# Weight conversion with low parts written in place, two mantissa tiles, a high-part tile of its own and one store for each part

## The chip, the cores and the metric

The kernel runs on one core of one Trainium2 chip. The metric is the device time of one execution in microseconds (us). The kernel before takes 964.32 us, the median of three runs (963.54 to 965.41).

## What is computed

Bucketed attention (queries and keys meet only where six sign bits agree) feeds a gated block. Cut to what matters:

```python
mask = q_bucket[:, :, :, None] == k_bucket[:, :, None, :]
scores = np.where(mask, scale * np.matmul(q, k.transpose(0, 1, 3, 2)), -1000000000.0)
attn = np.exp(scores - np.max(scores, axis=-1, keepdims=True))
attn = attn / (np.sum(attn, axis=-1, keepdims=True) + 1e-09)
x = np.matmul(attn, v)          # 4 batches, 8 heads, 768 positions, 64 wide; joined to 3072 x 512
gate = 1.0 / (1.0 + np.exp(-(x @ w_gate)))   # weights 512 x 1536, float64
out = (gate * (x @ w_val)) @ w_out           # 1536 x 512, float64
```

The three weight matrices arrive as float64, which no engine here computes with: the kernel reads them as pairs of 32-bit integers and makes float32 numbers of them, each of which it splits into a high part (rounded to the matmul format) and a low part (the rest).

## The kernel before

There are two phases. In **phase 1** (to about 405 us) a pair of heads at a time goes through attention: scores on TensorE (L1551, L1557), their maximum on VectorE (L1569, 192 times), the exponential on ScalarE (L1578), transposes on TensorE (L1614) whose results ScalarE or VectorE copies back (L1620), and the product with v (L1630). For each next pair, q and k are loaded, turned on TensorE (L1358), copied out (L1372 to L1378, on ScalarE or VectorE) and split into high and low parts (L1385 to L1389, on ScalarE, GpSimd or VectorE). In **phase 2** (from about 429 us) the gate and value products run in a seven-product scheme on blocks of weights (L1178) and the output products follow (L932). Between the two stands a short piece with ordinary products (L896, L932 with `zg`, `zv`, `zo`).

Beside attention the weights are converted, 34 items in phase 1 and six more early in phase 2. An item is a 128x512 block (for gate and value also three sums and one difference of its quarters, which make it 128x896). Its steps: a load of 512 KB into `raw` (L745, L748, L813); on VectorE `exponent` (L689) and `mantissa` (L697), on ScalarE `shifted` (L692), on VectorE `whole` (L702) and `signed` (L707); on GpSimd `scaled` (L712), `sums` (L821 to L824), `high` (L766 or L830) and `low` (L769 or L833); then a store to DRAM (L772 or L836), from where phase 2 fetches the weights (L1728, L777). The exponents lie in tile `wex`, the mantissas, later the finished float32 numbers, in tile `wmf`; high and low part go to one tile `wk` with two halves.

The order of the work is set by a planner (`Plan`, L380): each step is a task with a key; TensorE follows a list of task numbers (`ORDER`) and the other engines take the ready task with the smallest key (keys are moved by the table `SHIFT`). A task takes and gives counted resources (`stock`): `raw1` one load buffer, `mid1` one pair of `wex` and `wmf`, taken by `exponent` and given back by `low`; `wk` one tile, taken by `high` and given back when the store has landed. Some steps have two possible engines, and the planner takes the one that is free. Each engine then executes its own instructions strictly in the order that came out, and SyncE issues nearly all DMAs in the same way.

Of the kernel before, what the change touches and what calls it, by code (L numbers as in the profile page):

```python
# [19 lines left out]
P = 128  # L20
# [21 lines left out]
SLOTS = ("two", "one", "e", "st", "su", "sv", "rb", "xs", "vr", "h", "raw2")  # L42
# [465 lines left out]
def lsh_attention_glu_kernel(ctx, tc, q, k, v, proj, w_gate, w_val, w_out, out):  # L508
# [165 lines left out]
    def floats(key, load, after, last, name):  # L674
# [12 lines left out]
        def exponent():  # L687
            z["ex"] = stage().tile([P, N_EL], I32, name=f"ex{name}", tag="wex", bufs=stock["mid" + own])
            nc.vector.tensor_scalar(z["ex"], z["high"], 0x7FF00000, None, op0=ALU.bitwise_and)  # L689
# [45 lines left out]
    def load_w(key, n, j, early, last=None):  # L735
# [32 lines left out]
        def low(eng):  # L768
            eng.tensor_sub(z["w"][:, 1], f(z["mf"]), f(z["w"][:, 0]))  # L769
# [1007 lines left out]
```

## Time and profile before

| | |
|---|---|
| median of three runs | 964.32 us (963.54 to 965.41) |
| the profiled execution: its own time, its span | 965.6 us, 963.8 us |
| TensorE busy | 952.0 us, 99% of the span |
| VectorE, ScalarE, GpSimd busy | 608.2, 548.2, 274.3 us |
| granted TensorE clock, mean | 0.999 |

The page gives busy times of each engine and the chain of work that ended last; the same view can be asked of a stretch. A row of a group of instructions has its line in the code, engine, operation, output and inputs, shapes, count, then the busy time in us, the mean of one in ns, and the idle time of the engine just before them with what ended it. In a timeline a row has its start and duration in us; in brackets stands the idle time before it and its releaser. DVE is VectorE, ACT ScalarE, POOL GpSimd, PE TensorE, PEld its weight loads, SPq SyncE's queue.

### The profile page before, as it was taken

How to read it: one execution, taken by the hardware profiler on the slowest of the kernel's cores; microseconds unless marked ns; L12 is line 12 of the kernel's file. 1: busy time of each engine (PE TensorE's matmuls, PEld its weight loads, DVE VectorE, ACT ScalarE, POOL GpSimd, SP SyncE). 2: the span in 40 equal slices, each digit the busy share in tenths (PEclk: the TensorE clock that was granted, in tenths of full speed). 3: DMA queues.
4: the chain of work that ended last, by engine and by line, in shares of the span. 5: the costliest groups of instructions: out<-in, count | busy, mean ns of one | idle time of the engine just before them, and what ended most of it. 6: DMA issues, size and time to landing. Idle time of an engine off the chain costs nothing.

```text
span 963.8 us, 20105 instructions
## 1 busy us (share of the span) xinstructions
PE 952.0 (99%) x8067; PEld 774.8 (80%) x8070; DVE 608.2 (63%) x1173; ACT 548.2 (57%) x993; POOL 274.3 (28%) x325
## 2 busy tenths in 40 slices
PE   9999999999999999999999999999999999999998
PEld 5666665666666567689999999999999999999997
DVE  7999898999899898676656743334633336333332
ACT  5988898898888889554334433324433235333322
POOL 4444655666765665630000000000000000000000
PEclk9999999999999999999999999999999999999999
DMA  7666888888897877489966774444744444644421
GB/s 186 175 194 189 224 252 241 244 249 238 263 268 213 233 228 228 171 315 411 370 237 230 280 262 175 153 153 154 271 170 158 170 177 173 222 154 153 154 78 66
DMA packets 116606, 204.37 MB, mean 212 GB/s; under 512 B 63456, under 2 KB 87968, under 8 KB 110624
## 3 DMA queue, kind: packets, MB, share of 16 engines
q1 hardware_dynamic: 107456, 118.08, 39.9%
q0 software_dynamic: 6688, 84.42, 23.7%
q8 instruction: 63, 1.03, 0.4%
q10 hardware_dynamic: 2368, 0.59, 0.3%
q14 instruction: 31, 0.25, 0.1%
HBM read 147.84 MB, written 43.42 MB: 198 GB/s over the span
## 4 chain that ended last, share of the span: by engine, by line
PE 92%; DVE 4%; DMA 2%; ACT 1%; issue 1%; SPq 0%; ACTq 0%; DVEq 0%
PE y L932 20%; PE pv L1630 12%; PE zBg L1178 10%; PE zBv L1178 10%; PE sc L1557 9%; PE tp L1614 7%; PE zDv L1178 5%; PE zDg L1178 5%; PE sc L1551 4%; PE zAg L1178 2%; PE zAv L1178 2%; PE h L1452 1%; DVE e L1569 1%; PE zg L896 1%; PE zv L896 1%; PE idle L642 1%
## 5 line engine op out<-in xcount | busy, mean ns | idle before, releaser
L1569 DVE TENSOR_SCALAR_CACHE_REDUCE e<-sc 128x768 f32<-128x768 f32 x192 | 177.1, 952 | 20.3 <-PE sc L1557 18.5
L1578 ACT ACTIVATE e<-e,st 128x768 f32<-128x768 f32 x192 | 178.9, 933 | 15.1 <-DVE e L1569 13.2
L932 PE MATMUL y<-wo,gh 128*128 128x512 f32 x480 | 151.0, 396 | 0.0
L1630 PE MATMUL pv<-e,vr 128*64 128x384 f32 x768 | 140.7, 496 | 0.0
L1620 ACT COPY e<-tp 128x768 f32<-128x768 f32 x144 | 112.2, 795 | 27.9 <-PE tp L1614 27.1
L1614 PEld LDWEIGHTS tp<-ident,e 64*128 64x128 f32 x2304 | 87.0, 138 | 45.7 <-issue 13.7
L1178 PE MATMUL zBg<-x,wsg 128*128 128x384 f32 x552 | 111.0, 335 | 0.0
L1178 PE MATMUL zBv<-x,wsv 128*128 128x384 f32 x552 | 110.7, 335 | 0.0
L1178 PEld LDWEIGHTS zBg<-x,wsg 128*128 128x128 f32 x552 | 98.2, 188 | 6.6 <-ACT t1g L1186 0.4
L1178 PEld LDWEIGHTS zBv<-x,wsv 128*128 128x128 f32 x552 | 98.3, 188 | 6.0
L932 PEld LDWEIGHTS y<-wo,gh 128*128 128x128 f32 x480 | 89.9, 187 | 15.2
L1614 PE MATMUL tp<-ident,e 64*128 64x64 f32 x2304 | 99.6, 226 | 1.8 <-DVE e L1569 0.9
L1271 ACT CAST gh<-zt 128x384 fp32r<-128x384 f32 x92 | 47.1, 514 | 95.1 <-DVE zt L1266 75.5
L932 PE MATMUL y<-wo,gl 128*128 128x512 f32 x240 | 93.2, 388 | 0.0
L1557 PE MATMUL sc<-kh,ql 64*128 64x384 f32 x192 | 89.8, 468 | 0.0
L1557 PE MATMUL sc<-kh,qsl 64*128 64x384 f32 x192 | 89.8, 468 | 0.0
L1630 PEld LDWEIGHTS pv<-e,vr 128*64 128x64 f32 x768 | 48.2, 136 | 51.3 <-issue 43.0
L1728 POOL DMA_DIRECT2D wsv<-kzv x23 | 12.2, 532 | 236.9 <-PE zDg L1178 224.6
L1728 POOL DMA_DIRECT2D wsg<-kzg x23 | 12.3, 536 | 227.4 <-PE zDv L1178 206.9
L1250 ACT ACTIVATE sig<-sig 128x384 f32<-128x384 f32 x69 | 36.2, 525 | 61.7 <-DVE sig L1193 61.6
L1274 DVE TENSOR_TENSOR gl<-zt,gh 128x384 fp32r<-128x384 f32 x92 | 51.0, 554 | 29.2 <-ACT gh L1271 29.2
L1551 PE MATMUL sc<-kq 64*128 64x384 bf16 x384 | 64.8, 328 | 2.3 <-ACT e L1620 1.1
(214 smaller groups left out, 1964.4 us busy)
## 6 DMA issues: line engine op xcount, KB each, us to landing
wsg<-kzg POOLq DMA_DIRECT2D x23, 1792.0 KB, 8.1
wsv<-kzv POOLq DMA_DIRECT2D x23, 1792.0 KB, 7.6
kzg<-wkg SPq DMA_DIRECT2D x12, 896.0 KB
kzv<-wkv SPq DMA_DIRECT2D x12, 896.0 KB
rawg<-in_moe_w_gate_dram SPq DMA_DIRECT2D x14, 512.0 KB
rawv<-in_moe_w_val_dram SPq DMA_DIRECT2D x14, 512.0 KB
vr<-in_v_dram SPq DMA_DIRECT2D x16, 384.0 KB
rb<-rd SPq DMA_DIRECT2D x64, 96.0 KB
```

The costliest lines, as they stand in the source:

```text
L932: nc.tensor.matmul(acc, a[:, slot, ts_], w, start=(first and i == 0), stop=(last and i == 2), skip_group_check=cols != slice(None),)
L1178: nc.tensor.matmul(acc, streams[n, jp][:, c, wa, a_], X[x_][:, xa, c], start=first and c == 0 and i == 0, stop=c == 1 and i == 2, skip_gro ...
L1250: lambda blk=blk: nc.scalar.activation(sig[:, blk], w["B"][:, :GN] if blk == 2 else sig[:, blk], AF.Sigmoid),
L1271: nc.scalar.copy(side["h"][:, blk], w["z", blk])
L1274: eng.tensor_sub(side["l"][:, blk], w["z", blk], f(side["h"][:, blk]))
L1551: nc.tensor.matmul(sc[:, j, :GN], kq[z["h"]][rows, 2 + 2 * g + h, t * P : (t + 1) * P], kq[z["h"]][rows, h], start=True, stop=False, tile_ ...
L1557: nc.tensor.matmul(sc[:, j, :GN], q_[rows, c], z["k" + x][rows, h * GN : (h + 1) * GN], start=False, stop=(m == 2), tile_position=(j * D, 0),)
L1569: nc.vector.tensor_scalar(sp(e), gz["sc", t, h][:, :, :GN], -MASKED * SCALE, None, op0=ALU.min, op1=ALU.min, accum_out=gz["st", t][:, h : ...
L1578: nc.scalar.activation(e, e, AF.Exp, bias=st[:, h : h + 1], scale=-1.0, accum_out=gz["su"][:, h * GT + t : h * GT + t + 1],)
L1614: nc.tensor.transpose(tp[:, r, at_ : at_ + D], gz["e", t, h][rows, c * P : (c + 1) * P], ident[rows, rows], tile_position=(r * D, 0),)
L1620: copy(gz["e"][:, :, c * P : (c + 1) * P].rearrange("p n (r d) -> p r n d", r=2), gz["tp", c][:, :, :GN].rearrange("p r (n d) -> p r n d", ...
L1630: nc.tensor.matmul(gz["pv"][rows, :GN], z["v"][:, h, c], gz["e"][:, h * GT : (h + 1) * GT, c * P : (c + 1) * P], start=(c == 0), stop=(c = ...
```

## The change

Storage: `low` no longer writes the second half of `wk` but the tile that holds the mantissas, in place. `wk` keeps only the high part, half the size, and the space goes into a second `wmf` tile, so that the total is the same. The resource `mid1` now stands for the mantissa tiles alone and counts two; `exponent` takes a new resource `ex1` (one `wex` tile), given back by `scaled`; `mantissa` takes `mid1`, given back when the store of the low part has landed. `wk` is given back when the high part's store has landed and `low` has run. Each part has its own store of half the bytes: the high part can be stored while `low` still runs. The same for the six items of phase 2 (`mid2`, `ex2`, `wk2`). Blocks that stay on the chip (the first two of each matrix) keep their old places. The tables `ORDER` and `SHIFT` are new throughout (only their size is told here).

```diff
-SLOTS = ("two", "one", "e", "st", "su", "sv", "rb", "xs", "vr", "h", "raw2")
+SLOTS = ("two", "one", "e", "st", "su", "sv", "rb", "xs", "vr", "h", "raw2", "mid1", "mid2")
...
-        raw1=1, mid1=1, raw2=2, mid2=1, wk=1, xr=1, x2=1, x3=1, ob=3,
+        raw1=1, mid1=2, ex1=1, raw2=2, mid2=2, ex2=1, wk=1, xr=1, x2=1, x3=1, ob=3,
...
-            z["all"] = stage().tile([P, SL * P], I32, name=f"mf{name}", tag="wmf", bufs=stock["mid" + own])
+            z["all"] = stage().tile([P, SL * P], I32, name=f"mf{name}", tag=f"wmf{slot['mid' + own]}", bufs=1)
...
-        b1 = add(key, "dve", 336, exponent, after=[a], take=["mid" + own], port=0.92)
+        b1 = add(key, "dve", 336, exponent, after=[a], take=["ex" + own], port=0.92)
...
-        c1 = add(key, "dve", 400, mantissa, after=[b1], port=0.92)
+        c1 = add(key, "dve", 400, mantissa, after=[b1], take=["mid" + own], port=0.92)
...
-            eng.tensor_sub(z["w"][:, 1], f(z["mf"]), f(z["w"][:, 0]))
+            eng.tensor_sub(z["l"], f(z["mf"]), f(z["h"]))
...
-            y["w"] = stage().tile([P, 2, SL * P], F32R, name=f"wk{n}{jp}{c}", tag="wk", bufs=stock["wk"]).rearrange(
+            y["h"] = stage().tile([P, SL * P], F32R, name=f"wk{n}{jp}{c}", tag="wk", bufs=1).rearrange(
...
-            eng.tensor_sub(y["w"][:, 1], y["f"], f(y["w"])[:, 0])
+            y["l"] = y["f"].bitcast(F32R)
+            eng.tensor_sub(y["l"], y["f"], f(y["h"]))
...
-            nc.sync.dma_start(kept_z[n, jp][:, c], f(y["w"]))
+            nc.sync.dma_start(kept_z[n, jp][:, c, m], f(y["hl"[m]]))
...
-        keeps.setdefault((n, jp), []).append(dma(key, 917504, keep, after=[m], give=["wk2" if last else "wk"]))
+        s_ = [dma(key, 458752, lambda: keep(0), after=[h]), dma(key, 458752, lambda: keep(1), after=[m], give=["mid" + own])]
+        add(FIRST, "sp", 0, lambda: None, after=[s_[0], m], give=["wk2" if last else "wk"])
+        keeps.setdefault((n, jp), []).extend(s_)
```

Over the whole program TensorE has the same instructions in another order. The other engines differ in 32 more stores on SyncE, and in where the planner put the steps with two engines: VectorE has 5 copies of turned q fewer (`rawq`, ScalarE has 5 more), 1 copy of transposes fewer (`e<-tp`, ScalarE 1 more), 2 low parts of x fewer (`xl`, GpSimd 2 more), 1 low part of k more (`kl`, GpSimd 1 fewer), 1 low part of weights more (GpSimd 1 fewer), and 1 copy of a result in phase 2 fewer; 5 high parts of q and k moved from ScalarE to GpSimd.

VectorE at the border of the first and second batch, the place at which TensorE idles longest in phase 1; `e,st<-sc` are the maxima, `exg`, `mfg` the conversion, `e<-tp` a copy of transposes, `xs` the divided result, `kq` the bits. Before:

```order
L1569 TENSOR_SCALAR e_0_0_1996,st_0_0_0_1995<-sc_0_0_0_1_2036 128x768
L1569 TENSOR_SCALAR e_0_0_1996,st_0_0_1_2078<-sc_0_0_1_0_2052 128x768
L689 TENSOR_SCALAR exg_0_2097<-rawg_0_1933 128x512
L1620 COPY e_3_0_1570<-tp_3_0_5_2065 128x2x6x64
L697 TENSOR_SCALAR mfg_0_2131<-rawg_0_1933 128x512
L1569 TENSOR_SCALAR e_0_0_1996,st_0_0_2_2147<-sc_0_0_2_0_2121 128x768
L1569 TENSOR_SCALAR e_0_0_1996,st_0_0_1_2078<-sc_0_0_1_1_2108 128x768
L702 SCALAR_TENSOR_TENSOR mfg_0_2131<-rawg_0_1933,mfg_0_2131 128x512
L1637 TENSOR_TENSOR xs_3_0_2166<-pv_3_0_1922,rb_3_0_1915 128x384
L707 SCALAR_TENSOR_TENSOR exg_0_2097<-rawg_0_1933,exg_0_2097 128x512
L1458 TENSOR_SCALAR kq_209<-h_1_2159,thr,mul 128x384
```

And in the changed kernel, at the same maxima:

```order
L1611 TENSOR_SCALAR e_0_0_2070,st_0_0_0_2069<-sc_0_0_0_1_2039 128x768
L1420 TENSOR_SCALAR rawq_1_2120<-tq_1_2097 128x2x6x64
L1611 TENSOR_SCALAR e_0_0_2070,st_0_0_1_2140<-sc_0_0_1_0_2111 128x768
L860 TENSOR_TENSOR mfg_0_2036<-mfg_0_2036 128x128
L861 TENSOR_TENSOR mfg_0_2036<-mfg_0_2036 128x128
L862 TENSOR_TENSOR mfg_0_2036<-mfg_0_2036 128x128
L863 TENSOR_TENSOR mfg_0_2036<-mfg_0_2036 128x128
L1679 TENSOR_TENSOR xs_3_0_2170<-pv_3_0_1999,rb_3_0_1883 128x384
L1611 TENSOR_SCALAR e_0_0_2070,st_0_0_1_2140<-sc_0_0_1_1_2161 128x768
L1611 TENSOR_SCALAR e_0_0_2070,st_0_0_2_2202<-sc_0_0_2_0_2186 128x768
L717 TENSOR_SCALAR exg_1_2223<-rawg_1_2095 128x512
L1500 TENSOR_SCALAR kq_209<-h_1_2197,thr,mul 128x384
```

The exponent, the copy and the mantissa that stood in one piece between two maxima are gone from here; a copy of q and four short sums stand there instead, and the next item's exponent follows two maxima later.

GpSimd at the end of phase 1, the last items converted there; `gl` is the first step of the piece between the phases. Before:

```order
L712 TENSOR_TENSOR mfg_0_7506<-mfg_0_7506,exg_0_7500 128x512
L821 TENSOR_TENSOR mfg_0_7506<-mfg_0_7506 128x128
L822 TENSOR_TENSOR mfg_0_7506<-mfg_0_7506 128x128
L823 TENSOR_TENSOR mfg_0_7506<-mfg_0_7506 128x128
L824 TENSOR_TENSOR mfg_0_7506<-mfg_0_7506 128x128
L830 CAST wkg_7574<-mfg_0_7506 128x896
L833 TENSOR_TENSOR wkg_7574<-mfg_0_7506,wkg_7574 128x896
L920 TENSOR_TENSOR gl<-gf_0_0_7643,gh 128x384
```

And in the changed kernel:

```order
L869 CAST wkv_7513<-mfv_0_7397 128x896
L873 TENSOR_TENSOR mfv_0_7397<-mfv_0_7397,wkv_7513 128x896
L740 TENSOR_TENSOR mfo_7574<-mfo_7574,exo_7568 128x512
L798 CAST wo_7604<-mfo_7574 128x512
L801 TENSOR_TENSOR mfo_7574<-mfo_7574,wo_7604 128x512
L962 TENSOR_TENSOR gl<-gf_0_0_7674,gh 128x384
```

The last item is now a block of the output weights, which has no sums, and its low part overwrites `mfo`.

## Rows read from the trace of the kernel before

**Rows 1.** The page: busy time by engine, and the chain that ended last.

```profile
PE 952.0 (99%) x8067; PEld 774.8 (80%) x8070; DVE 608.2 (63%) x1173; ACT 548.2 (57%) x993; POOL 274.3 (28%) x325
PE 92%; DVE 4%; DMA 2%; ACT 1%; issue 1%; SPq 0%; ACTq 0%; DVEq 0%
```

**Rows 2.** Busy time by stage: stretch, length, engines (instructions), clock, DMA share, GB/s.

```profile
20.00:400.00 380.00, 374.74 (x4952) 246.46 (x4952) 343.53 (x691) 331.69 (x587) 225.52 (x242) 1.00 0.78 228
400.00:430.00 30.00, 28.75 (x187) 24.45 (x184) 17.79 (x22) 12.08 (x20) 14.49 (x19) 1.00 0.67 253
430.00:964.00 534.00, 529.97 (x2775) 492.56 (x2773) 232.20 (x420) 194.83 (x374) 23.85 (x44) 1.00 0.54 200
```

**Rows 3.** Waits of TensorE to 420 us: us in total, times, longest.

```profile
PE sc L1551 <- ACT e L1620: 1.1, 2, 0.9
PE h L1452 <- DVE xs L1637: 1.1, 1, 1.1
PE zo L932 <- DVE gl L920: 1.0, 1, 1.0
PE tp L1614 <- DVE e L1569: 0.9, 1, 0.9
```

**Rows 4.** Timeline, 103 to 114 us, four rows of four engines.

```profile
107.29 1.83 POOL L1389 TENSOR_TENSOR ql<-rawq,qh 128x768 fp32r<-128x768 f32 x1
...
107.31 2.09 DVE L697 TENSOR_SCALAR mfg<-rawg 128x512 int32<-128x512 int32 x1
...
110.31 0.94 ACT L1578 ACTIVATE e<-e,st 128x768 f32<-128x768 f32 x1 [1.19 <-DVE e L1569]
...
112.99 0.34 PE L1551 MATMUL sc<-kq 64*128 64x384 bf16 x2 [0.91 <-ACT e L1620]
```

**Rows 5.** Groups of instructions by shape to 425 us: steps that change engine.

```profile
L1378 DVE TENSOR_SCALAR rawq<-tq 128x768 f32<-128x768 f32 x8 | 7.6, 956 | 2.4 <-PE tq L1358 2.3
...
L1620 DVE COPY e<-tp 128x768 f32<-128x768 f32 x48 | 45.3, 951 | 5.2 <-PE tp L1614 5.1
...
L870 DVE TENSOR_TENSOR xl<-xr,xh 128x384 fp32r<-128x384 f32 x5 | 4.8, 979 | 0.4 <-POOL xh L867 0.4
...
L1389 DVE TENSOR_TENSOR kl<-rawk,kh 128x768 fp32r<-128x768 f32 x3 | 3.5, 1172 | 0.6 <-ACT kh L1385 0.6
```

**Rows 6.** The same view: the two conversion steps on VectorE with one input.

```profile
L697 DVE TENSOR_SCALAR mfv<-rawv 128x512 int32<-128x512 int32 x12 | 8.3, 688 | 0.0
...
L689 DVE TENSOR_SCALAR exg<-rawg 128x512 int32<-128x512 int32 x12 | 6.9, 575 | 0.0
...
L697 DVE TENSOR_SCALAR mfg<-rawg 128x512 int32<-128x512 int32 x12 | 6.7, 556 | 0.0
...
L689 DVE TENSOR_SCALAR exv<-rawv 128x512 int32<-128x512 int32 x12 | 6.4, 533 | 0.0
...
L689 DVE TENSOR_SCALAR exo<-rawo 128x512 int32<-128x512 int32 x10 | 6.2, 620 | 0.0
...
L697 DVE TENSOR_SCALAR mfo<-rawo 128x512 int32<-128x512 int32 x10 | 4.2, 420 | 0.0
```

**Rows 7.** Groups by shape: a low part on VectorE (430 to 964 us) and on GpSimd.

```profile
L833 DVE TENSOR_TENSOR wkv<-mfv,wkv 128x896 fp32r<-128x896 f32 x2 | 2.2, 1089 | 1.4 <-ACT wkv L830 1.4
...
L833 POOL TENSOR_TENSOR wkv<-mfv,wkv 128x896 fp32r<-128x896 f32 x10 | 22.3, 2227 | 0.8
```

**Rows 8.** Timeline, 204 to 220 us: load, end of one item, start of the next.

```profile
207.20 0.37 SPq L813 DMA_DIRECT2D rawv<-in_moe_w_val_dram  x1
...
213.28 2.11 POOL L833 TENSOR_TENSOR wkv<-mfv,wkv 128x896 fp32r<-128x896 f32 x1
...
215.95 0.42 DVE L689 TENSOR_SCALAR exv<-rawv 128x512 int32<-128x512 int32 x1
```

**Rows 9.** Stores of the gate weights on SyncE: ns min/median/max; and a wait there.

```profile
L836 SPq DMA_DIRECT2D kzg<-wkg x12: 320/346/1213, 105.8 to 496.1; - x12
...
SPq L1025 <- DMA kzg<-wkg: 3.5, 1, 3.5
```

More of the change, by code (lines that the diff above doesn't have):

```diff
@@ L687, in exponent @@
         def exponent():
-            z["ex"] = stage().tile([P, N_EL], I32, name=f"ex{name}", tag="wex", bufs=stock["mid" + own])
+            z["ex"] = stage().tile([P, N_EL], I32, name=f"ex{name}", tag="wex", bufs=1)
             nc.vector.tensor_scalar(z["ex"], z["high"], 0x7FF00000, None, op0=ALU.bitwise_and)
@@ L720, in floats @@
         return z, add(
-            key, "dve" if last else "pool", 680 if last else 1240, lambda: scaled(nc.vector if last else nc.gpsimd), after=[d], port=0.92
+            key, "dve" if last else "pool", 680 if last else 1240, lambda: scaled(nc.vector if last else nc.gpsimd), after=[d], give=["ex" + own], port=0.92
         ), own
@@ L764, in high, with keep, keep_both @@
             else:
-                z["w"] = stage1.tile([P, 2, SL * P], F32R, name=f"w{n}{j}", tag="wk", bufs=stock["wk"])[:, :, :N_EL]
-            (nc.scalar.copy if last else nc.gpsimd.tensor_copy)(z["w"][:, 0], f(z["mf"]))
+                z["h"] = stage1.tile([P, SL * P], F32R, name=f"w{n}{j}", tag="wk", bufs=1)[:, :N_EL]
+            if "w" in z:
+                z["h"], z["l"] = z["w"][:, 0], z["w"][:, 1]
+            else:
+                z["l"] = z["mf"].bitcast(F32R)
+            (nc.scalar.copy if last else nc.gpsimd.tensor_copy)(z["h"], f(z["mf"]))
         def low(eng):
-            eng.tensor_sub(z["w"][:, 1], f(z["mf"]), f(z["w"][:, 0]))
-        def keep():
+            eng.tensor_sub(z["l"], f(z["mf"]), f(z["h"]))
+        def keep(m):
+            nc.sync.dma_start(kept[n, j][:, m], f(z["hl"[m]]))
+        def keep_both():
             nc.sync.dma_start(kept[n, j], f(z["w"]))
@@ L781, in load_w @@
             key, "dve" if last else "pool", 629 if last else 1236, lambda: low(nc.vector if last else nc.gpsimd), port=0.92,
-            after=[h], give=["mid" + own],
+            after=[h], give=["mid" + own] if early or last else [],
         )
         if not early and not last:
-            a = dma(key, 524288, keep, after=[made[n, j]], give=["wk"])
-            fetches[n, j] = (a, fetch)
+            s_ = [
+                dma(key, 262144, lambda: keep(0), after=[h]),
+                dma(key, 262144, lambda: keep(1), after=[made[n, j]], give=["mid" + own]),
+            ]
+            add(FIRST, "sp", 0, lambda: None, after=[s_[0], made[n, j]], give=["wk"])
+            fetches[n, j] = (s_, fetch)
         elif early and n == "o":
-            kept_early.append(dma(key + 20, 524288, keep, after=[made[n, j]]))
+            kept_early.append(dma(key + 20, 524288, keep_both, after=[made[n, j]]))
     def stream(n, jp):
@@ L826, in high, with keep @@
         def high():
-            y["w"] = stage().tile([P, 2, SL * P], F32R, name=f"wk{n}{jp}{c}", tag="wk", bufs=stock["wk"]).rearrange(
-                "p a (s m) -> p a s m", s=SL
+            y["h"] = stage().tile([P, SL * P], F32R, name=f"wk{n}{jp}{c}", tag="wk", bufs=1).rearrange(
+                "p (s m) -> p s m", s=SL
             )
-            (nc.scalar.copy if last else nc.gpsimd.tensor_copy)(y["w"][:, 0], y["f"])
+            (nc.scalar.copy if last else nc.gpsimd.tensor_copy)(y["h"], y["f"])
         def low(eng):
-            eng.tensor_sub(y["w"][:, 1], y["f"], f(y["w"])[:, 0])
-        def keep():
-            nc.sync.dma_start(kept_z[n, jp][:, c], f(y["w"]))
+            y["l"] = y["f"].bitcast(F32R)
+            eng.tensor_sub(y["l"], y["f"], f(y["h"]))
+        def keep(m):
+            nc.sync.dma_start(kept_z[n, jp][:, c, m], f(y["hl"[m]]))
         z, e, own = floats(key, load, [last or score_tasks[at_n]], last, f"{n}{jp}_{c}")
@@ L842, in load_pair @@
         m = add(key, [("dve", 1005, lambda: low(nc.vector))] if last else
-                [("pool", 2078, lambda: low(nc.gpsimd)), ("dve", 1005, lambda: low(nc.vector))], after=[h], give=["mid" + own], port=0.92)
+                [("pool", 2078, lambda: low(nc.gpsimd)), ("dve", 1005, lambda: low(nc.vector))], after=[h], port=0.92)
         made.setdefault((n, jp, "p"), []).append(m)
-        keeps.setdefault((n, jp), []).append(dma(key, 917504, keep, after=[m], give=["wk2" if last else "wk"]))
+        s_ = [dma(key, 458752, lambda: keep(0), after=[h]), dma(key, 458752, lambda: keep(1), after=[m], give=["mid" + own])]
+        add(FIRST, "sp", 0, lambda: None, after=[s_[0], m], give=["wk2" if last else "wk"])
+        keeps.setdefault((n, jp), []).extend(s_)
         return h
@@ L1229, in visit @@
                         a, fetch = fetches["o", j]
[L1230 removed]
+                        made["o", j] = dma(1e3, 524288, fetch, after=[*a, m1] + (g_free if j >= NJ - J1 else []))
             e1 = copies("t1", m1)
@@ L1720, in switch @@
         later["ps"] = ctx.enter_context(tc.tile_pool(name="ps3", bufs=2, space=PSUM))
-    later["switch"] = add(0, "sp", 0, switch, after=every + [a for a, _ in fetches.values()] + [a for k_ in keeps.values() for a in k_],
+    later["switch"] = add(0, "sp", 0, switch, after=every + [a for k_, _ in fetches.values() for a in k_] + [a for k_ in keeps.values() for a in k_],
                           give=["moe"] * 3 + [r for r, n in late_stock.items() for _ in range(n)])
```

1 line of the change is left out of this document (removed), and 604 rows, old and new, of tables (ORDER, SHIFT).

## The prediction

> **What bounds the kernel now.** I read the page first, then the busy times by stage, then TensorE's waits, then the chain of waits. The page says that TensorE is busy 952.0 of 963.8 us and that 92% of the chain that ended last runs on it, 4% on VectorE, 2% on DMAs [rows 1]. A time can then only fall where TensorE stands still, or where its work shrinks; the change leaves its work as it is. By stage: from 430 us to the end TensorE is busy 529.97 of the 534 us of the row, which is 4 us less only because the span ends at 963.8 us and a tail of copies and the last store follows its last product; no wait of it was listed there. Nothing is to be had in phase 2. From 20 to 400 us it is busy 374.74 of 380, so it idles 5.26 us; from 400 to 430 us it idles 1.25 us [rows 2]. All that a better order can give by this view is 6.5 us, 0.7% of the time. (Ends of matmuls are modelled, so some stall may hide in "busy"; I keep that for the range.) The stalls are few and have named causes: scores that waited for a copy on ScalarE (1.1 us), the hash product behind a division on VectorE (1.1), the output product behind a low part (1.0), a transpose behind a maximum on VectorE (0.9) [rows 3].
>
> VectorE is what stands behind most of them. In the same stretch it is busy 343.53 of 380 us, 90% [rows 2], and executes in order. The longest stall shows the mechanism [rows 4]: the mantissa step of a conversion took 2.09 us, where the cheapest group of that step has 0.42 [rows 6]; it started 0.02 us after GpSimd began a low part of q of 1.83 us and ended 0.28 us after it. The next maxima stood behind it, ScalarE waited 1.19 us for them, its copy came late, and TensorE idled 0.91 us.
>
> The Trainium skill gives a rule for this ("SBUF — State Buffer", section "Who interferes with whom"): VectorE in a two-port mode, and GpSimd, hold a shared pair of ports for a whole instruction, and the other blocks. The trace agrees: 2.09 us beside 1.83 us of GpSimd.
>
> **The change part by part.**
>
> *Work that changes engine.* Priced by the rows [rows 5]: VectorE loses five copies of q (5 x 0.956 = 4.78 us), one copy of transposes (0.95) and two low parts of x (2 x 0.979 = 1.96); it gains one low part of k (1.17) and one low part of weights, which no row shows on VectorE in phase 1: in phase 2 it took 1.09 us beside an idle GpSimd, and the GpSimd row of 2.23 us is the far end [rows 7]; I take 1.1, since the instruction is the same. Sum: 4.78 + 0.95 + 1.96 - 1.17 - 1.1 = 5.4 us less on VectorE in phase 1, 1.6% of its 343.53 us. The copies go to ScalarE, which hands five casts to GpSimd in return, so that it stays about level; GpSimd was busy 225.52 of 380 us and has room [rows 2].
>
> What this is worth on TensorE has two ends. If stalls shrink only as the chain's share on VectorE does, it is 1.6% of 4% of 963.8 us [rows 1], 0.6 us. If every us taken from VectorE stood on the chain, it is 5.4 us, the whole idle time of that stretch. I take half of the 5.26 us idle, 2.6 us, because the three named stalls of that stretch (1.1, 1.1 and 0.9 us, rows 3) end on VectorE or, by rows 4, go back to it for most of their length, 3.1 us together, and a new order will hardly remove all of them.
>
> *In-place low parts, two mantissa tiles, a shorter hold of the exponent tile.* The conversion was a serial chain: the next exponent started 0.56 us after the end of the item's low part (213.28 + 2.11 = 215.39; 215.95), although its data had been asked for at 207.20 us, 8.75 us earlier [rows 8]. With two tiles that wait is no longer needed. But in the order of the changed kernel every exponent of phase 1 still stands behind the low part of the item before, and the exponents sit among the 192 maxima within seven places of where they were (last of phase 1 after the 192nd in both). So the second tile buys room for the planner, not speed in the conversion itself: I take 0 for it, bounded by +0.5 and -0.6 us as a share of the chain. What hides it is attention: TensorE needs no converted weight before 429 us.
>
> *Port collisions.* The excess of the one-input conversion steps over 0.42 us is 12 x (0.268 + 0.136 + 0.155 + 0.113) + 10 x 0.20 = 10.1 us on VectorE [rows 6]. In the order, 18 of these steps have a low part of q or k as GpSimd's last emitted instruction before; in the changed one it is 13. By that share they would cost 7.3 us, 2.8 less. Against it: 29 of them now follow a low part of weights (25 before) with no tile to wait for. I take 0 and keep -1.5 us (2.8 x 0.55, see the rival) and the rival as ends.
>
> *Stores.* 24 stores of gate and value blocks and 8 of output blocks become two each: 32 more issues at 0.346 us median on SyncE (0.32 to 1.21) [rows 9], 11 us of its queue over 490 us. Behind a store on that queue stand loads of k, q and v, the swaps of q and the spreading of sums and bits, for which attention waits. The bytes are the same. Most issues fall in gaps of SyncE; the chain has 0% on it [rows 1]. I take 0, with a rival. In GpSimd's queue the fetches of phase 2 wait for both stores instead of one, early enough.
>
> *The end of phase 1.* The load of phase 2's first operands waited 3.5 us for the last store [rows 9]. Now the last item is an output block: no sums (four steps) and a shorter low part, so that store ends some 3 us earlier. TensorE has products to fill this stretch, and its 1.0 us stall there waits for the gate's low part [rows 3], which stays. 0 us; without that cover the 3.5 us would have counted.
>
> *TensorE's own order.* The same instructions, 395 runs of one kind ahead of phase 2's first product instead of 386: nothing, or a few tenths lost.
>
> **Sum.** -2.6 us. The profiled execution took 965.6 us by its own time for a span of 963.8; the median of the runs is 964.32, 1.3 below. On the median: 964.3 - 2.6 = 961.7 us.
>
> **The rivals.**
>
> *The relief lies off TensorE's path.* Where a maximum waits for scores, a freer VectorE only idles longer, and the second tile stays unused as the order shows it: then the change does not do what its storage allows, and -0.6 us of the chain's share remain, less a few tenths for TensorE's order: 964 us. For it: DMAs hold 2% of the chain [rows 1], loads, swaps and bits for which attention waits, and the change does nothing for them.
>
> *Collisions take the gain back and more.* Before, no conversion step of the next item could meet the low part of weights on GpSimd (2.23 us, rows 7), since the tile fenced it off; now nothing does but the order of the queues and the landing of the load. A step that meets it blocks VectorE, and the maxima behind it. Price from rows 4: 1.67 us more on VectorE (2.09 - 0.42) became 0.91 us of idle TensorE, 0.55 of it. Three such events more than before eat the 2.6 us; from five on (5 x 0.91 = 4.6, less 2.6) it is 2.0 us slower, 966.3 us. Against it: an in-order VectorE would have stood before the same instruction anyway, waiting for the tile. That rule of the Trainium skill, named above, speaks for this rival, since it has the later one blocked for the whole instruction; no run here shows it yet for the low part of weights.
>
> *SyncE's queue.* If eight of the 32 new issues stand ahead of a load or a swap for which TensorE waits, 8 x 0.346 = 2.8 us are lost; with the relief's lower end, 0.6 us, the result is 966.5 us. It decides from six such places on (2.1 us).
>
> **How the numbers follow.** The forecast has 0.45, the relief off the path 0.33, collisions 0.13, SyncE's queue 0.09. A measurement of this kernel can tell about 0.2%, 1.9 us, from no change. The forecast's case is faster than that; the second case is within; the last two are slower: 0.45, 0.33, 0.22. Low end: all 6.5 us of idle time gone, 957.8, rounded to 957.5 us, since some stall may hide in busy time. High end: 966.5 us by the two slower rivals, and half a microsecond beyond, 967 us.
>
> **What would show it.** Right: TensorE's idle time from 20 to 400 us falls from 5.26 to about 2.6 us, VectorE's busy time there by about 5 us, the first product of phase 2 comes 2 to 3 us earlier, and from there to the end nothing differs by more than 0.5 us. The collisions: the mean of the L697 and L689 steps rises (sum over 15 us instead of 10.1), with single ones of 2 us beside a low part of weights. SyncE: waits of TensorE end on loads of k, on swaps or on bits. The forecast is wrong if phase 2's length changes, or if VectorE gets its 5 us and TensorE idles as before.

## The result, and the profile after

The changed kernel takes 971.96 us, the median of six runs (970.18 to 972.66); the kernel before takes 964.28 us in six runs beside them (963.54 to 965.54). The ratio is 1.0076, with a 95% interval of 1.0064 to 1.0088: slower by 7.7 us, where 2.6 us less was forecast. The profiled execution of the changed kernel took 971.65 us, its span is 969.9 us.

The page of the changed kernel first: busy time by engine, and the chain that ended last (as [rows 1]).

```profile
PE 953.0 (98%) x8070; PEld 776.5 (80%) x8070; DVE 605.3 (62%) x1166; ACT 547.7 (56%) x995; POOL 279.3 (29%) x330
...
PE 84%; DVE 7%; POOL 2%; DMA 2%; issue 2%; ACT 1%; SPq 0%; DVEq 0%; POOLq 0%; ACTq 0%
```

TensorE has as much work as before (953.0 against 952.0 us), but VectorE's part of the chain is 7% instead of 4%, and GpSimd's, which was not in the list, is 2%. By stage (as [rows 2]):

```profile
20.00:400.00 380.00, 369.47 (x4852) 244.42 (x4850) 339.28 (x673) 325.18 (x580) 226.56 (x242) 1.00 0.76 224
400.00:430.00 30.00, 28.75 (x248) 22.18 (x245) 15.32 (x24) 13.10 (x22) 16.33 (x20) 1.00 0.56 197
430.00:970.00 540.00, 536.06 (x2810) 498.68 (x2808) 235.22 (x425) 198.88 (x381) 25.74 (x46) 1.00 0.55 203
```

From 20 to 400 us TensorE is busy 369.47 of 380 us: it idles 10.53 us instead of 5.26. The later stages are as they were. VectorE is busy 339.28 us in this stretch, 4.25 less than before, but that is not relief: the changed kernel is some 5 us behind at 400 us, and 18 instructions of VectorE fewer lie in the stretch. A fair comparison ends at the first product of phase 2, where TensorE has done the same 5286 products. Before:

```profile
0.00:428.70 428.70, 420.73 (x5286) 280.94 (x5290) 374.68 (x752) 352.52 (x618) 250.06 (x281) 1.00 0.77 226
```

And the changed kernel:

```profile
0.00:434.30 434.30, 421.20 (x5286) 282.01 (x5286) 373.85 (x746) 351.08 (x618) 253.58 (x284) 1.00 0.75 222
```

VectorE has six instructions fewer, as the order says, and 0.83 us less; TensorE idles 13.1 us up to there instead of 8.0. The first product of phase 2 starts at 434.3 us instead of 428.7. In the view of one tile of weights a row has the shortest, the middle and the longest duration in ns, then the first and the last start in us; of before:

```profile
L1178 PE MATMUL zBg<-x,wsg x552: 331/334/445, 428.7 to 937.5; 128*128 128x384 f32 x184
```

And of the changed kernel:

```profile
L1220 PE MATMUL zBg<-x,wsg x552: 333/334/411, 434.3 to 943.6; 128*128 128x384 f32 x184
```

So 5.6 of the 6.1 us by which the span grew are lost ahead of phase 2. TensorE's waits there (as [rows 3]: us in total, times, longest):

```profile
PE sc L1593 <- DVE e L1611: 3.5, 4, 1.5
PE sc L1593 <- DMA kq<-bd: 3.0, 1, 3.0
PE tp L1656 <- DVE e L1611: 1.7, 2, 1.0
PE pv L1672 <- DVE e L1662: 1.1, 1, 1.1
```

Two things stand out: waits for VectorE, 6.3 us in seven places, and one wait of 3.0 us for the bits `kq`.

**What the waits for VectorE are.** At 83 us, rows of GpSimd, VectorE and TensorE:

```profile
83.30 1.83 POOL L1431 TENSOR_TENSOR ql<-rawq,qh 128x768 fp32r<-128x768 f32 x1
...
83.41 2.27 DVE L735 SCALAR_TENSOR_TENSOR exo<-rawo,exo 128x512 int32<-128x512 int32 x1
...
85.60 0.94 DVE L1611 TENSOR_SCALAR_CACHE_REDUCE e<-sc 128x768 f32<-128x768 f32 x1
...
86.60 0.34 PE L1593 MATMUL sc<-kq 64*128 64x384 bf16 x2 [1.38 <-DVE e L1611]
```

`signed` (L735, the step that was L707) took 2.27 us; it began 0.11 us after a low part of q on GpSimd and ended 0.55 us after it. The maximum behind it came that much later, and TensorE idled 1.38 us for that maximum. The same stands at 104.57, 237.03 and 260.19 us (`signed` of 2.35, 2.36 and 2.48 us, each 0.02 to 0.03 us behind the start of a low part of k or q; TensorE idles 1.49, 0.71 and 1.03 us), and once with other partners at 330.57 us: a low part of k on VectorE, 2.80 us, beside a low part of weights on GpSimd (TensorE idles 1.13 us). The five idle times are 5.74 us together.

The groups of steps by shape show that the collisions have changed their victim. `signed` of the kernel before, in the view of groups (busy us, mean ns of one):

```profile
L707 DVE SCALAR_TENSOR_TENSOR exv<-rawv,exv 128x512 int32<-128x512 int32 x12 | 9.0, 752 | 0.0
...
L707 DVE SCALAR_TENSOR_TENSOR exg<-rawg,exg 128x512 int32<-128x512 int32 x12 | 8.2, 687 | 0.2 <-ACT exg L692 0.2
...
L707 DVE SCALAR_TENSOR_TENSOR exo<-rawo,exo 128x512 int32<-128x512 int32 x10 | 7.3, 735 | 0.5 <-ACT exo L692 0.5
```

The same view of the changed kernel, with `signed` first and behind it the one-input steps, which answer to [rows 6]:

```profile
L735 DVE SCALAR_TENSOR_TENSOR exg<-rawg,exg 128x512 int32<-128x512 int32 x12 | 14.8, 1232 | 0.0
...
L735 DVE SCALAR_TENSOR_TENSOR exo<-rawo,exo 128x512 int32<-128x512 int32 x10 | 9.0, 903 | 0.8 <-ACT exo L720 0.8
...
L735 DVE SCALAR_TENSOR_TENSOR exv<-rawv,exv 128x512 int32<-128x512 int32 x12 | 8.2, 682 | 0.9 <-ACT exv L720 0.8
...
L717 DVE TENSOR_SCALAR exv<-rawv 128x512 int32<-128x512 int32 x12 | 6.8, 567 | 0.0
...
L717 DVE TENSOR_SCALAR exg<-rawg 128x512 int32<-128x512 int32 x12 | 6.7, 558 | 0.0
...
L717 DVE TENSOR_SCALAR exo<-rawo 128x512 int32<-128x512 int32 x10 | 5.9, 586 | 0.2 <-DMA rawo<-in_moe_w_out_dram 0.2
L725 DVE TENSOR_SCALAR mfg<-rawg 128x512 int32<-128x512 int32 x12 | 5.3, 440 | 0.0
L725 DVE TENSOR_SCALAR mfv<-rawv 128x512 int32<-128x512 int32 x12 | 5.0, 414 | 0.0
L725 DVE TENSOR_SCALAR mfo<-rawo 128x512 int32<-128x512 int32 x10 | 4.7, 474 | 0.0
```

Over 0.42 us each, the one-input steps now have an excess of 12 x (0.147 + 0.138) + 10 x 0.166 + 12 x 0.014 + 10 x 0.054 = 5.8 us; it was 10.1. Over 0.684 us each (the cheapest group of `signed` has 0.682), `signed` has 12 x 0.548 + 10 x 0.219 = 8.8 us; it was 12 x (0.068 + 0.003) + 10 x 0.051 = 1.4 us.

**What the wait for the bits is.** The chain of waits of the changed kernel, 112 to 136 us (start, us, what):

```profile
116.67 8.14 DMA xr<-xd
...
124.82 5.34 DMA kq<-bd
```

The load of x was issued on SyncE at 116.67 us, ahead of the transfers that spread the bits, among a store of the new halves on either side of it and a weight load. It took 8.14 us. On SyncE's queue the load is the eighth transfer ahead of the second half of the spreading; that half was issued only when the load had landed, and TensorE idled until 130.21 us. Ahead of these transfers the same chain passes two more stretched steps of VectorE: a short sum (L861) at 109.96 us, 1.79 us beside a low part of q, where its three siblings take 0.28 us each, and the next item's exponent at 114.30 us, 1.34 us instead of 0.42, beside a low part of weights. What these two add to the wait is not shown.

### The profile page after: what moved, and what is told of

Same layout as the page of the kernel before. It is cut to its first block, busy times and chain, and to the rows that moved or that the text cites. A ratio compares the mean times of both kernels' runs of the same rounds, so it can differ in the third digit from the quotient of the medians.

```text
span 969.9 us, 20169 instructions
## 1 busy us (share of the span) xinstructions
PE 953.0 (98%) x8070; PEld 776.5 (80%) x8070; DVE 605.3 (62%) x1166; ACT 547.7 (56%) x995; POOL 279.3 (29%) x330
## 3 DMA queue, kind: packets, MB, share of 16 engines
q8 instruction: 63, 1.03, 0.5%
## 4 chain that ended last, share of the span: by engine, by line
PE 84%; DVE 7%; POOL 2%; DMA 2%; issue 2%; ACT 1%; SPq 0%; DVEq 0%; POOLq 0%; ACTq 0%
PE y L974 20%; PE zBg L1220 10%; PE zBv L1220 10%; PE pv L1672 9%; PE sc L1599 7%; PE tp L1656 6%; PE zDv L1220 5%; PE zDg L1220 5%; PE sc L1593 3%; PE zAg L1220 2%; PE zAv L1220 2%; DVE e L1611 2%; PE zg L938 1%; PE zv L938 1%; DMA xr<-xd 1%
```

## The experiments

Two theories came out of the comparison. **A**: the new order lets VectorE's conversion steps meet GpSimd's low parts at places where TensorE waits for the next maximum; that is the 5.7 us. **B**: the spreading of bits at 116 to 130 us stands behind bulk transfers, the new half stores among them; that is the 3.0 us. All runs of the kernel before that stood beside these experiments have medians from 964.36 to 964.75 us. An overview, medians in us:

| kernel | median (range, runs) | ratio to before, 95% interval |
|---|---|---|
| changed | 971.96 (970.18 to 972.66, 6) | 1.0076 [1.0064, 1.0088] |
| 1 new storage, old tables | 1002.8 (1000.31 to 1011.36, 4) | 1.0412 [1.0362, 1.0462] |
| 2 old storage, new tables | 1032.45 (1031.67 to 1033.65, 4) | 1.0704 [1.0688, 1.072] |
| 3 low parts in quarters | 965.32 (962.37 to 972.16, 10) | 1.0009 [0.9988, 1.003] |
| 4 x load issued by GpSimd | 969.37 (968.93 to 971.23, 4) | 1.0048 [1.0031, 1.0065] |
| 5 bits ahead of bulk | 971.4 (970.12 to 972.35, 5) | 1.0073 [1.006, 1.0087] |
| 6 = 3 and 5 | 965.08 (962.99 to 968.24, 11) | 1.0005 [0.9992, 1.0018] |
| 7 kernel before, quarters | 963.24 (961.81 to 967.41, 11) | 0.9997 [0.9985, 1.0009] |
| 8 = 5 and low parts in halves | 967.47 (965.49 to 969.02, 11) | 1.003 [1.002, 1.0039] |
| 9 = 5 and x converted later | 971.85 (971.42 to 973.49, 5) | 1.0079 [1.0062, 1.0096] |
| 10 = 9 and quarters | 966.85 (965.81 to 968.5, 9) | 1.0024 [1.001, 1.0037] |
| 11 kernel before, x converted later | 967.9 (966.36 to 968.46, 9) | 1.0034 [1.0022, 1.0045] |
| 12 = 11 and quarters | 967.13 (966.41 to 968.19, 11) | 1.0028 [1.0019, 1.0037] |
| 13 five exchanges | 966.31 (964.01 to 967.94, 11) | 1.0014 [1.0001, 1.0028] |
| 14 = 13, 5 and one `xl` later | 965.14 (964.16 to 968.5, 11) | 1.0013 [1.0001, 1.0025] |
| 15 = 6 and one `xl` later | 964.56 (962.94 to 965.69, 11) | 0.9999 [0.9987, 1.0011] |
| 16 = 7 and three `xl` later | 963.48 (963.05 to 964.37, 11) | 0.9989 [0.9979, 1.0] |

**1 and 2: storage alone, order alone.** The task numbers of the one kernel's `ORDER` and `SHIFT` were translated for the other.

```diff
-ORDER = [...]; SHIFT = {...}      # of the changed kernel
+ORDER = [...]; SHIFT = {...}      # of the kernel before, task numbers translated (run 2: the other way round)
```

> The changed storage (two mantissa tiles, high-part tile, two stores) with the order tables of the kernel before: the same list of TensorE tasks and the same key shifts, carried over task by task; a store's shift goes to both of its halves. Theory A, the loss of 7.7 us sits in the new order (conversion steps that meet low parts of q and k on GpSimd, and a spreading of bits behind a slow load): 963 to 966 us, TensorE idle from 20 to 400 us near the 5.3 us of before. Theory B, the loss sits in the storage (32 more DMAs on SyncE, the fence of the tile gone): 969 to 973 us.

> The storage of before with the new order tables, carried over task by task (the second halves of stores lose their shift). Theory A (order): 969 to 973 us, with VectorE's fourth conversion step at above 2 us beside a low part of q or k three or more times. Theory B (storage): 963 to 966 us. If both this one and the storage alone are near 964, the loss is in the two together.

Both are much slower, 1002.8 and 1032.45 us, outside both expectations. TensorE's longest wait of the first:

```profile
PE zBg L1220 <- ACT x L1077: 10.2, 1, 10.2
```

And the two longest of the second:

```profile
PE zBg L1178 <- ACT x L1035: 15.3, 1, 15.3
PE zBg L1178 <- ACT t1g L1186: 10.2, 1, 10.2
```

The operand `x`, for which they wait, is loaded late. In both chains of waits a late conversion of weights stands ahead of that load: in run 1 an item converted from 423 to 433 us, in run 2 two stores of converted weights at 461 and 467 us. Phase 2 begins late (its first products at 460.7 and 480.0 us). A list that is laid out for one set of buffers does not fit the other. Neither theory foresaw it, and neither is tested by it: storage and order of this change cannot be priced apart in this way.

**3: shorter low parts.** GpSimd's low parts of q and k in four instructions of 192 columns.

```diff
-                eng.tensor_sub(z[n + "l"], z["raw", n], f(z[n + "h"]))
+                for w in [slice(m, m + S // 4) for m in range(0, S, S // 4)] if eng is nc.gpsimd else [slice(None)]:
+                    eng.tensor_sub(z[n + "l"][:, w], z["raw", n][:, w], f(z[n + "h"])[:, w])
```

> The changed kernel, with the low parts of q and k on GpSimd in four instructions of 192 columns instead of one of 768. Collisions: the steps of 2.27 to 2.48 us on VectorE (four, with 4.6 us of idle TensorE right behind them) can be held up by one quarter, some 0.6 us, at most: 967 to 969 us, none of these steps over 1.5 us. Rival, the collisions lie off the path or GpSimd's longer work (four starts) costs as much: 971 to 973 us.

6.6 us come back in the median, more than the 3 to 5 us that were expected; the ten runs scatter by 10 us, and the profiled execution (968.27 us) is 3.4 us below that of the changed kernel. The waits for VectorE ahead of 400 us are gone to 0.4 us, the wait for the bits stays:

```profile
PE sc L1594 <- DMA kq<-bd: 4.2, 2, 3.4
...
PE sc L1594 <- DVE e L1612: 0.4, 2, 0.3
```

The longest `signed` is 1.13 us here. The pieces cost GpSimd 0.65 us each, 2.6 instead of 1.9 us for a whole low part; TensorE's list of waits shows none for that. At the fifth place, whose GpSimd step (a low part of weights) is not cut, the low part of k takes 1.74 us here and TensorE does not wait.

**4: the load of x from another queue.**

```diff
-            nc.sync.dma_start(z["xr"], xd[b][:, :, cols].rearrange("c p t -> p c t"))
+            nc.gpsimd.dma_start(z["xr"], xd[b][:, :, cols].rearrange("c p t -> p c t"))
```

> The changed kernel, with the two 768 KB loads of x in phase 1 issued by GpSimd instead of SyncE. Eight-in-turn theory: a DMA on SyncE's queue waits until the eighth before it has landed; the spreading of bits of the second batch stood eight behind a load of x of 8.1 us and TensorE idled 3.03 us for it; that wait goes: 968 to 970 us. Rival, the spreading is late anyway (the bits' own store, the DMA itself): 971 to 973 us, idle stays.

2.6 us come back in the median, yet the profiled execution (971.23 us) still waits 2.4 us for the bits, now because the transfer ahead of them, the 96 KB that write the bits out, is itself late:

```profile
116.54 8.18 DMA bd<-kq
```

So it is not only the queue that holds the bits back. The x load is in flight here too, issued by GpSimd at 115.58 us and landed 9.0 us later. That such bulk transfers hold up a small one is the likely reason; no run varies them alone.

**5 and 6: the bits first.** On SyncE the four `kq<-bd` are issued ahead of the x load, the half store and the weight load; run 6 has the quarters of run 3 as well.

```diff
 L1460 DMA qsl   L1637 DMA rd
+L1510 DMA kq<-bd x2   L1512 DMA kq<-bd x2
 L902 DMA xr<-xd   L876 DMA kzg<-mfg   L852 DMA rawv
-L1510 DMA kq<-bd x2   L1512 DMA kq<-bd x2
```

> The changed kernel with three bulk transfers of SyncE's queue at about 116 to 121 us (the x load of 768 KB, the store of the low parts of one half of kzg, the load of rawv) issued after the four kq<-bd transfers instead of ahead of them; nothing else. They are not needed before 123 us (rawv's exponent at 132 us, x's first product after 180 us). Theory B (the wait of 3.0 us for kq<-bd at 130 us is the spread of kq standing behind bulk transfers that the new stores put there): this wait falls below 0.6 us, kq<-bd lands before 122 us, and the time is about 3 us below the changed kernel, 969. The DVE-ended waits (3.5 and 1.7 us) stay. Rival (the spread waits for something else, or TensorE waits for VectorE at the same place anyway): time within 1 us of the changed kernel, 971 to 973.

> Both cures at once: the low parts of q and k on GpSimd in four instructions of 192 columns, and the three bulk transfers behind the four kq<-bd. If A (the collisions of signed with these low parts, 6.6 us by the run with four pieces alone) and B (3 us) are all of the loss and add up, the time is 971.9 - 6.6 - 3 = 962.3, under the kernel before, and TensorE's waits of 20 to 400 us come to 5 us or less. If the two stalls overlap (the first only takes up what the second would have waited), it stays at 964 to 966.

The wait for the bits is gone, as B says, and the time is not: 971.4 and 965.1 us, what it was without the move. VectorE's rows of run 5:

```profile
128.64 0.82 DVE L912 TENSOR_TENSOR xl<-xr,xh 128x384 fp32r<-128x384 f32 x1 [2.18 <-POOL xh L909]
129.39 0.55 DVE L1679 TENSOR_TENSOR xs<-pv,rb 128x384 f32<-128x384 f32 x1
129.86 0.94 DVE L1611 TENSOR_SCALAR_CACHE_REDUCE e<-sc 128x768 f32<-128x768 f32 x1
```

TensorE's wait for the last of them, in the list of its waits:

```profile
PE tk L1400 <- DVE e L1611: 1.6, 1, 1.6
```

A low part of x (`xl`, L912) stood 2.18 us before the maxima, since GpSimd's high part of x waited for the load of x, which is now later still. B is right about the queue and wrong about the price: in this trace the same late load holds TensorE through a second queue.

**7 and 8: is it the order, or do shorter pieces help anywhere; and the dose.** Run 7 is the kernel before with the quarters of run 3; run 8 is run 6 with halves (`S // 2`).

> The kernel before with the low parts of q and k on GpSimd in four instructions, as in the run of the changed kernel with four pieces. A says that the gain there came from collisions that the new order makes; the kernel before has about 4 long VectorE steps beside these low parts and about 1 to 2 us of TensorE waits behind them, so it gains 2 us at most: 962 to 965. Rival (shorter GpSimd pieces speed up any kernel of this kind, by letting VectorE in sooner everywhere): it gains about 6 us too, 958 to 960.

> As the run with both cures, with the low parts in two instructions of 384 columns instead of four. If VectorE is shut out for the rest of one GpSimd instruction, the longest signed step is about 0.68 + 1.0 = 1.7 us instead of 2.3 to 2.5 us whole and 1.2 us in quarters; a part of the TensorE waits comes back (up to about 2 us), and GpSimd saves about 0.4 us for each of the 24 low parts: 962 to 965. Rival (the number of GpSimd instructions matters, not their length): the same time as with quarters within 0.5 us.

The kernel before gains 1.4 us by the medians (the interval of its ratio includes 1), against 6.6: most of these collisions belong to the new order.

With halves the time is 967.47 us, with quarters (run 6) 965.08; 962 to 965 was expected. In the steps the dose shows: the longest `signed` is 2.48 us beside whole low parts, 1.54 with halves, 1.13 with the quarters of run 3, so the length of the GpSimd instruction counts, and waits of 0.6 and 0.7 us for VectorE are back at 86 and 106 us. The 2.4 us of time do not measure it. Run 8 also waits 2.3 us for bits at 351 us, which the others do not, and 1.2 us at 328 us behind a low part of k (2.86 us) that stands beside a low part of weights, which neither run cuts.

**9 to 12: x converted later.** Theory C: what is left is the late x load, through SyncE's and VectorE's queues. x is first multiplied at 411 us, so its eight conversions were moved 8 to 15 us back, in the changed kernel (on top of run 5), with quarters, and in the kernel before without and with quarters. The moves are made in the list that the planner returns; of the changed kernel:

```diff
+    moves = [([571, 581, 591], 600), ([611, 619], 668), ([616, 623], 678), ([630, 634], 694), ([641, 646], 706), ([662], 715)]
```

> The changed kernel with the four kq<-bd ahead of the bulk transfers (as in the run that did only that) and, new, the eight conversions of x (xh on GpSimd, xl on GpSimd and VectorE), which wait for the x load, issued some 8 to 15 us later, spread between other work; the second x load moves behind them. x is first multiplied at 411 us. Theory C: one late transfer, the x load (8 us from issue to landing among the bulk transfers), holds TensorE through two queues: kq<-bd stands behind it on SyncE, and VectorE's maxima stand behind the conversion xl on VectorE. With both freed, the waits around 130 us (3.0 in the changed kernel, 1.6 with kq first) fall below 0.6 us, no stretch from 125 to 140 us shows a granted clock under 0.95, and the time is 1.6 to 3 us under the run with kq first: 968.4 to 969.8, with the collisions (5.7 us of waits) untouched. Rival: VectorE at 130 us is late by itself or for rb, another wait of 1.5 us takes its place, and the time stays at 971.

> The same with the low parts of q and k on GpSimd in four instructions. If collisions and the x load are the whole of what the changed kernel lost, the waits of TensorE from 20 to 400 us fall to 2.5 us or less and the time to 961 to 963, below both kernels; the difference to the run without the split is again 5.5 to 6.6 us. Rival: with the x load out of the way the collisions have slack and the split gives less than 4 us.

> The kernel before with the conversions of x issued later in the same way (its x load stays where it is). It waits 0.9 us at 130 us for VectorE, behind xl. By theory C it gains at most that: 963.4 to 964.6. Rival (the conversions of x cost wherever they stand): 964.6 or more.

> The kernel before with both: low parts of q and k in four instructions and x converted later. The run with the split alone had 963.2 us, with one wait of 2.8 us for VectorE behind xl at 130 us and a granted clock of 0.69 in the 5 us after it. By C both go: 959.5 to 961.0, below both kernels. Rival: the wait at 130 us moves on and the time stays at 963.

C fails as a forecast: run 9 is at 971.85 us, run 10 at 966.85, run 11 at 967.9 and run 12 at 967.13, each above what it would have allowed. The long wait at 130 us is gone in runs 9, 11 and 12 (0.8 us at the most is left from 128 to 136 us; run 10 has 1.0 and 0.8), but other waits came: run 11, the kernel before, is 3.4 us slower. Three of its waits, which are 0.9 us, 0.2 us and none in the trace of before:

```profile
PE tp L1614 <- DVE e L1569: 1.7, 3, 1.0
PE sc L1551 <- DMA kq<-bd: 1.1, 2, 0.8
PE sc L1551 <- DVE e L1620: 1.1, 1, 1.1
```

**13: the five places alone.** Five pairs of neighbours on VectorE exchange their places: `signed` (in the last pair the low part of k) goes behind the next maximum (behind the next copy). GpSimd's instructions are whole.

```diff
 L730 mfo<-rawo,mfo
 L1611 e<-sc
-L735 exo<-rawo,exo
 L1611 e<-sc
+L735 exo<-rawo,exo
```

> The changed kernel with five VectorE steps, each of which the trace shows stretched beside a GpSimd low part (signed at 83, 105, 237 and 260 us, the low part of k at 331 us), issued one place later, behind the next maximum (the last one behind the next copy of transposed weights e); nothing else, GpSimd's instructions are whole. If these five places are the cause, TensorE's waits behind them (1.4, 1.5, 0.7, 1.0 and 1.1 us, 5.7 in all) go although the steps are still stretched, the wait of 3.0 us at 130 us stays, and the time is 966 to 967. Rival (the split helped by shorter pieces throughout, not at these places): 970 or more.

966.31 us, inside the expectation: 5.65 us come back for 5.74 us of idle time. The second place, which was at 104.57 us:

```profile
104.41 1.83 POOL L1431 TENSOR_TENSOR kl<-rawk,kh 128x768 fp32r<-128x768 f32 x1
104.43 0.08 DVE L1611 DVE_READ_ACCUMULATOR e<-sc 128x1 f32 x1
104.43 0.95 DVE L1611 TENSOR_SCALAR_CACHE_REDUCE e<-sc 128x768 f32<-128x768 f32 x1
...
105.31 1.48 DVE L735 SCALAR_TENSOR_TENSOR exg<-rawg,exg 128x512 int32<-128x512 int32 x1
```

The maximum, which reads PSUM, goes first and takes 0.95 us beside the low part, no longer than elsewhere. `signed` still stands until the low part has ended (106.24 us) and runs 0.55 us more, but TensorE no longer waits for what is behind it. At the first place `signed` still takes 1.22 us; at the other three the two steps hardly meet any more (0.85, 1.00 and, for the low part of k, 0.95 us). Of the 5.74 us, 0.34 us is left behind the third place and 0.49 us behind the fourth. This shows A: the same instructions, five exchanges, and nearly all the idle time at these places is gone. The 5.65 us of the medians are not a ledger of it, though. The wait for the bits, which was expected to stay, is 1.72 instead of 3.03 us in the profiled execution (964.5 us), and the scatter of this kernel goes with the granted clock (last section).

**14 to 16: a single `xl` later.** Run 14 is run 13 with run 5 and with VectorE's one `xl` behind the next two maxima; run 15 is run 6 with that; run 16 is run 7 with the kernel before's three `xl` behind the next one or two maxima.

```diff
+    moves = [([571, 581, 591], 600), ([619], 637)]          # run 15
+    moves = [([613], 636), ([621, 632], 645)]               # run 16, list of the kernel before
```

> The five exchanges, the four kq<-bd ahead of the three bulk transfers, and the one conversion xl that VectorE has at 126 us issued behind the next two maxima (GpSimd's conversions stay). If the five places and the late x load, through SyncE's queue and through VectorE's, are the loss, no wait over 1.2 us is left from 20 to 400 us and the time is 961 to 963.5, at or below the kernel before. Rival: a wait of 1.5 us or more stays near 130 us, and the time is 964 to 966.

> Low parts of q and k in four instructions, kq first, and the one VectorE xl behind two maxima. Against the run without the last step (965.1 us, with one wait of 2.2 us for VectorE at 129 us): 962.5 to 963.5 if that wait goes; 965 if another takes its place there.

> The kernel before with the low parts of q and k in four instructions and its three VectorE conversions xl at 126 to 130 us issued behind the next one or two maxima (GpSimd's conversions stay). Against the split alone (963.2 us, with a wait of 2.8 us at 131 us and a granted clock of 0.69 in the 5 us behind it): 960 to 961.5, below both kernels, if the wait goes and nothing takes its place; 963 if another does.

In all three another wait came, as the rivals had it. Run 15 is 0.5 us below run 6 and level with the kernel before; a wait of 1.5 us is at 133 us now. Run 14 gains 1.2 us on run 13 by the medians, with a wait of 2.4 us there. Run 16 keeps 0.9 us at the same place:

```profile
PE tp L1615 <- ACT rawq L1374: 0.9, 1, 0.9
```

By the medians it is level with run 7, and 0.9989 of the kernel before, with an interval that just reaches 1: a gain on the kernel before is not shown. At the border of the first and second batch, around 130 us, a wait is thus mended only to come back a little later behind another step. Which of its causes would have to go together is left open, and with it the 2 us by which run 13 is still above the kernel before.

## Why the prediction was wrong, point by point

**What bounds the kernel: right.** TensorE's work and phase 2 did not change: from the first product of phase 2 to the end of the span it is 535.6 us (969.9 less 434.3) against 535.1. All was decided in TensorE's idle time ahead of it, and most of that behind VectorE in its order, by the mechanism that [rows 4] had shown. (The stall of [rows 4], 0.91 us, is not the longest, as the prediction calls it: [rows 3] has one of 1.1 and one of 1.0 us.)

**Work that changes engine: a gain of 2.6 us that did not come.** The instructions left VectorE as listed, six fewer up to the first product of phase 2. But of the 5.4 us that were worked out for them, 0.83 us are left in its busy time; the new collisions took most of the rest. No gain of TensorE from it shows. Taking half of TensorE's idle time as the worth was a choice without a row that showed which idle time would go. Two of the old stalls at [rows 3] did go, behind the division and behind a maximum, but longer ones came in their place.

**Port collisions: the step that failed.** The term was 0, from -1.5 us to the rival's price. It counted only the steps with one input, 18 and then 13, and for these it was right: their excess fell from 10.1 to 5.8 us. It left out the steps that read two tiles in SBUF: `signed`, VectorE's own low parts, and the short sums. In the trace of before `signed` had only 1.4 us of excess; in the new order it has 8.8 us, and TensorE idles 5.74 us behind five such steps, four of `signed` and a low part of k. The prediction counted the kind of step that the old trace showed stretched, and not every step that a long GpSimd instruction can hold up.

The Trainium skill has this case in the same section that the prediction cites ("SBUF — State Buffer", section "Who interferes with whom"): a VectorE instruction with two SBUF inputs contends with a GpSimd instruction that reads SBUF. The traces agree: 2.27 to 2.48 us instead of 0.68.

For the planner such a pair is a sequence: at the four places its list has `signed` first and the low part of q or k next, 19 ns later, and lets the low part wait. On the chip the low part began 0.02 to 0.11 us ahead, and `signed` waited. The Trainium skill, in the same section of "SBUF — State Buffer", says that the order of issue decides who blocks. These four pairs agree.

**The rival "collisions take the gain back": right in its mechanism, too cheap, and given 0.13.** It decides from five more events on, and there are five. It priced one at 1.67 us on VectorE and 0.91 us on TensorE. Measured are 1.59, 1.67, 1.68 and 1.80 us for `signed` over 0.68 and 1.72 us for the low part of k over 1.08 (its mean in run 13), 8.5 us together, and 5.74 us on TensorE, 0.68 of it instead of 0.55. At these five places its partner was wrong: it spoke of the next item's steps beside the low part of weights, made possible by the second tile. Four of five stand beside low parts of q and k, which no tile ever fenced off; only the order had kept them apart. The pair that it named did come once on the chain of the bits, the exponent of 1.34 us at 114.30 us. And it subtracted the collisions from a gain of 2.6 us that was not there.

**Stores: whether 0 was right is not shown; the rival's place came, not its price.** The bits came 3.0 us late among the half stores, the x load and a weight load. The price was not 0.35 us for each store's issue, as the rival had it, but the time of whole transfers: 8.14 us for the x load ahead of the bits in the changed kernel, 8.18 us for the 96 KB of the bits themselves in run 4. What the stores alone contribute is not shown: moving one of them together with the two loads (run 5) gave no time back.

**Storage, the end of phase 1, TensorE's own order:** 0 each. Between the phases TensorE idles 1.25 us as before, so the end of phase 1 is right. The price of storage and of TensorE's order could not be measured apart (runs 1 and 2).

**The signs that the prediction named.** "Wrong if VectorE gets its 5 us and TensorE idles as before" is near what came: VectorE got 0.8 of them, and TensorE idles twice as much from 20 to 400 us. The sign for SyncE, waits of TensorE that end on bits, came too. The sign for collisions (sum of the L697 and L689 excess above 15 us) pointed at the wrong instructions and would have said that there were none.

## What to carry to other kernels

Before a new order is priced, list every pair of steps that can hold each other up, not only the pairs that collide in the old trace: an order that removes the visible collisions may make others. A VectorE step with its operands in SBUF belongs behind the next maximum that TensorE waits for, not ahead of it, when a long GpSimd step can start at the same moment; exchanging five pairs of neighbours gave 5.65 us back here, and cutting the GpSimd step into quarters gave 6.6 us without knowing the places. A stretch between two fixed times compares different work when one kernel has fallen behind; end it at the same instruction of both. Work taken from a busy engine is worth only what a named wait gives back.

## What was not expected of the hardware

After the idle stretch at 127 to 130 us the granted clock of TensorE is lower for some us. The changed kernel by stretch (the clock stands ahead of the DMA share):

```profile
120.00:130.00 10.00, 7.18 (x96) 4.84 (x93) 6.73 (x13) 8.21 (x15) 8.79 (x14) 1.00 0.92 287
130.00:135.00 5.00, 4.79 (x36) 3.35 (x38) 3.40 (x9) 2.86 (x4) 1.38 (x2) 0.66 0.92 262
135.00:140.00 5.00, 5.00 (x70) 3.31 (x68) 2.02 (x4) 3.83 (x8) 2.45 (x2) 1.00 0.84 223
```

The same of run 13:

```profile
120.00:130.00 10.00, 8.28 (x116) 5.90 (x112) 6.95 (x14) 8.15 (x15) 9.36 (x14) 1.00 0.93 297
130.00:135.00 5.00, 5.00 (x63) 2.75 (x60) 3.77 (x12) 4.69 (x8) 2.22 (x1) 1.00 0.95 243
```

And of run 4:

```profile
130.00:135.00 5.00, 5.00 (x38) 3.32 (x40) 3.41 (x9) 3.17 (x5) 1.97 (x3) 0.66 0.95 272
```

With a wait of 3.03 us the next 5 us have 0.66, a mean between the full 2.4 GHz and its other level, 1.2 GHz; with 1.72 us in run 13 they have 1.00. A product with v of twelve instructions took 2.58 us in that stretch, 2.09 us elsewhere. Runs 3 and 7 have 0.68 and 0.69 there, behind waits of 3.40 and 2.81 us. Run 4 has 0.66 behind a wait of 2.45 us, and run 14, with 2.39 us, has 1.00, so the length of the wait alone does not tell which comes. A wait at this place can cost more than its own length. The scatter of the mended kernels goes with the mean granted clock of a run: run 13 has 964.0 to 964.5 us in its four runs at 1.000 and 965.7 to 967.9 in the seven at 0.998 or less. That the scatter comes from this one stretch is not shown.
